# The second products of an expert layer turned: w2 stationary, 512 tokens moving, and the sum over experts kept transposed

## The chip, the cores and the metric

The kernel runs on one core of one Trainium2 chip. The metric is device time in microseconds (us), the median of the runs of one kernel. Engines carry the profile's names: PE is TensorE, DVE VectorE, ACT ScalarE, POOL GpSimd, SP the engine that issues most transfers.

## The reference

Three layers follow one another. The change touches the middle one, a mixture of E = 8 experts over N = 3072 tokens of width D = 384, with an inner width F = 1024; the gates P come from eight rounds of row and column scaling.

```python
def _moe_ref(x, w_gate, w1, w2):
    logits = x @ w_gate
    P = np.exp(logits - logits.max())
    for _ in range(8):
        P /= P.sum(1, keepdims=True) + 1e-09
        P /= P.sum(0, keepdims=True) + 1e-09
        P *= N / E
    for e in range(E):
        h = np.maximum(x @ w1[e], 0.0)
        ye = h @ w2[e]
        out += P[:, e:e + 1] * ye
```

Ahead of it stands a decaying linear attention (4 x 8 heads, 768 steps, head size 48), whose output is x; behind it a bilinear layer, `(x @ w_a) * (x @ w_b) @ w_out`, with an inner width of 1536.

## The kernel before

Every large product is made of float32 halves: an operand is split into a high part (a copy rounded to `F32R`) and a low part (the rest), and three matmuls high x high, high x low, low x high are added in PSUM.

The program has two parts. In the first, the attention of 24 steps of 128 tokens runs, and the gaps on PE are filled with expert 0 (`expert0`, seven of its eight 128-wide blocks, 256 tokens at a time, twelve batches); its result goes to DRAM as `y0`. In the second part, six phases of 1024 tokens follow: three of the expert layer (phases 0, 1, 2, here called the MoE phases) and three of the bilinear layer. An MoE phase has 19 jobs. A job takes three 128-wide blocks of the inner width through both products:

- `front` makes h = relu(x @ w1) for 2 x 512 tokens by a fast scheme of fifteen chains of three matmuls (w1 stationary, 512 tokens moving, line 975). Partial results are copied out of PSUM by ACT or combined by DVE (`pG`, `pF`, `z`).
- `halve` splits h into its two parts (`er`); ACT writes the high part, DVE or POOL the low one.
- `back` makes h @ w2 for all blocks of one expert that are pending, 22 calls a phase. Here h is stationary (128 x 128) and w2 moves (384 columns), so that the result has tokens on partitions: eight tiles of 128 tokens, each 3 matmuls a block (`gemm_t`, line 348, PSUM tile `pR`, three banks). DVE then adds it to `acc`, with the gate as a scalar of its partition (`scalar=prob[:, t, e:e+1]`).
- The accumulators start as `y0` times the gate of expert 0 (ACT). After the last expert, `x2` transposes each `acc` tile on PE (three matmuls), ACT copies it, and it goes to DRAM as `xd[1]` for the bilinear layer.

POOL splits the weights of the first product in phase 0 (`w1_split`, later phases load the split weights from DRAM), does part of the `halve` work, and makes sums of x (`x_make`). DVE also converts the float64 weights of the bilinear layer (`convert`, 60 pieces of seven DVE operations; `CONVERTS` says which jobs do how many). The gates (`sinkhorn`) are made at the start of phase 0, between its first products.

All work of the second part goes into a `Plan`: each piece has a priority, an engine, a cost by hand and the keys that it reads and writes, and the order on each engine is fixed by playing these through before the program is built. Engines take their own instructions strictly in that order.

Of the kernel before, what the change touches and what calls it, by code (L numbers as in the profile page):

```python
# [189 lines left out]
def kernel(  # L190
# [479 lines left out]
    def expert0(plan, b, prio, nm, bufs, fill, part=None):  # L670
# [20 lines left out]
        ws = ftiles(w_e0[0][1]) + ftiles(w_e0[1][1])  # L691
        for tt in range(EB // 128) if part != 0 else ():
# [28 lines left out]
    def sinkhorn(plan, prio, rounds, bank):  # L721
# [161 lines left out]
    def x_take(plan, prio, ph, i, eng, tmp):  # L883
# [6 lines left out]
        plan.add(prio + 5, ACT, .6, [kt, *(guard[:1] if i >= NX - 5 else [])], [f"xs{i}"], partial(nc.scalar.activation, out=xh, in_=t, func=AF.Copy))  # L890
# [19 lines left out]
    used.update(F=0, R=0)  # L910
# [4 lines left out]
    b_z = ring("z", 19, [128, TB], sbb)  # L915
# [3 lines left out]
    cut["at"] = sum(2 * KD * 128 * m for m in e0_f)  # L919
# [4 lines left out]
    acc = ring("acc", TPG, [128, DM], sbb)  # L924
# [24 lines left out]
    most = {(0, 1), (0, 2), (1, 1), (1, 2)}  # L949
    on_pool = {"moe": ({(1, 2)}, most, most), "out": ((), most | {(0, 0), (1, 0)}, most | {(0, 0), (1, 0)})}  # L950

    def front(n):
# [258 lines left out]
```

## Time and profile before

| | |
|---|---|
| median of 3 runs | 2205.8 us (2205.55 to 2208.18) |
| profiled execution, span | 2207.7 us (no time of its own is given beside the span; it lies inside the runs) |
| PE busy | 2173.2 us, 98% |
| DVE busy | 1613.6 us, 73% |
| ACT busy | 942.6 us, 43% |
| POOL busy | 906.7 us, 41% |

Busy shares are means over stages with different limits. A busy PE means that a matmul is in flight, since matmuls overlap; how fast they follow one another is read from starts in the timeline. The first part (attention and the fill) ends at 425.6 us; the MoE phases start at 425.6, 867.2 and 1318.2 us, the bilinear layer at 1766.2 us, each with the first matmul of its first job.

### The profile page before, as it was taken

The page shows a single profiled execution, that of the slowest core. Times are in us where ns is not written, and L with a number is a line of the kernel's source. Part 1 is how long each engine was busy: PE and PEld are TensorE (multiplying, and loading weights), DVE is VectorE, ACT ScalarE, POOL GpSimd, SP SyncE. Part 2 cuts the span into 40 slices and gives each one's busy share as a digit, 9 for nine tenths or more (in the row PEclk, how much of TensorE's full clock was granted, in tenths as well). Part 3 has the DMA queues.
Part 4 walks back from the last instruction along what each step waited for, and adds up shares of the span by engine and source line. Part 5 has one row for each costly group of instructions (what it writes and reads, how often), then busy time and mean ns, then how long its engine had stood idle before and what let it go on. Part 6 is the DMA issues. An engine that isn't in the chain of part 4 may idle for free.

```text
span 2207.7 us, 41959 instructions
## 1 busy us (share of the span) xinstructions
PE 2173.2 (98%) x15933; PEld 1967.3 (89%) x15933; DVE 1613.6 (73%) x2904; ACT 942.6 (43%) x1785; POOL 906.7 (41%) x921
## 2 busy tenths in 40 slices
PE   8999999989999999999999999999999999999999
PEld 8999999969899999889999998899999988888888
DVE  6878888387778778767786687777766866776755
ACT  3444454454444444533334345333333545433432
POOL 2212121277776665332322244343222677444512
PEclk9999999999999999999999999999999999999999
DMA  7556663466665557864544558666544546787642
GB/s 133 109 104 162 165 126 81 135 216 220 222 229 184 203 194 278 299 231 141 194 152 152 175 203 275 210 222 211 176 138 162 163 172 226 254 276 229 235 164 72
DMA packets 325354, 413.43 MB, mean 187 GB/s; under 512 B 146976, under 2 KB 217248, under 8 KB 321696
## 3 DMA queue, kind: packets, MB, share of 16 engines
q1 hardware_dynamic: 302832, 393.97, 55.9%
q10 hardware_dynamic: 22320, 16.78, 2.3%
q8 instruction: 125, 2.05, 0.4%
q14 instruction: 77, 0.63, 0.1%
HBM read 279.33 MB, written 126.62 MB: 184 GB/s over the span
## 4 chain that ended last, share of the span: by engine, by line
PE 85%; DVE 5%; DMA 4%; POOL 3%; issue 1%; SPq 1%; ACT 1%; ACTq 0%; POOLq 0%; DVEq 0%
PE pR L348 35%; PE pG L975 24%; PE pF L975 9%; PE pM L336 4%; PE pM L348 3%; PE pT L462 1%; POOL stage L1170 1%; DVE z L1170 1%; PE pA L505 1%; PE pO L590 1%; PE pO L618 1%; DMA stage<-in_moe_w_dram 1%; PE pA L549 1%; PE pA L517 1%; DVE er L1170 1%
## 5 line engine op out<-in xcount | busy, mean ns | idle before, releaser
L348 PE MATMUL pR<-er 128*128 128x384 f32 x5052 | 1022.5, 338 | 1.6 <-ACT l L686 1.1
L348 PEld LDWEIGHTS pR<-er 128*128 128x128 f32 x5052 | 907.5, 189 | 75.5 <-ACT l L686 1.5
L1170 POOL TENSOR_TENSOR er<-z,er 128x512 fp32r<-128x512 f32 x221 | 294.7, 1347 | 655.8 <-ACT er L1170 396.5
L1170 ACT ACTIVATE z<-pG 128x512 f32<-128x512 f32 x474 | 282.7, 597 | 577.9 <-PE pG L975 452.1
L975 PE MATMUL pG<-xsh,w 128*128 128x512 f32 x1134 | 440.9, 395 | 7.9 <-ACT z L1170 6.6
L1170 DVE SCALAR_TENSOR_TENSOR acc<-pR,prob,acc 128x384 f32<-128x384 f32 x528 | 319.4, 612 | 113.3 <-PE pR L348 111.0
L1170 ACT ACTIVATE er<-z 128x512 fp32r<-128x512 f32 x420 | 250.6, 626 | 222.8 <-PE pR L348 167.9
L1170 DVE TENSOR_TENSOR z<-pF,z 128x512 f32<-128x512 f32 x324 | 221.6, 687 | 121.4 <-PE pF L975 82.9
L975 PE MATMUL pG<-er,w 128*128 128x512 f32 x972 | 278.8, 396 | 3.5 <-DVE z L1170 3.4
L1170 DVE TENSOR_TENSOR z<-z,pG 128x512 f32<-128x512 f32 x243 | 166.6, 686 | 125.3 <-PE pG L975 121.8
L975 PEld LDWEIGHTS pG<-xsh,w 128*128 128x128 f32 x1134 | 212.7, 188 | 45.3 <-ACT z L1170 11.7
L975 PE MATMUL pG<-xsl,w 128*128 128x512 f32 x567 | 224.1, 395 | 0.0
L975 PEld LDWEIGHTS pG<-er,w 128*128 128x128 f32 x972 | 179.0, 188 | 28.8 <-DVE z L1170 6.8
L688 POOL TENSOR_TENSOR er<-l,er 128x256 fp32r<-128x256 f32 x84 | 75.2, 897 | 281.1 <-ACT l L686 248.8
L1170 DVE TENSOR_TENSOR z<-pG,z 128x512 f32<-128x512 f32 x174 | 119.7, 688 | 84.8 <-PE pG L975 82.0
L1170 DVE SCALAR_TENSOR_TENSOR er<-z,er 128x512 fp32r<-128x512 f32 x171 | 166.7, 981 | 6.0 <-ACT er L1170 3.2
L1170 POOL TENSOR_TENSOR stage<-stage 128x128 f32<-128x128 f32 x325 | 160.1, 524 | 25.7 <-DMA stage<-in_moe_w_dram 17.2
L1170 POOL TENSOR_TENSOR w<-stage,w 128x768 fp32r<-128x768 f32 (+2 forms) x75 | 124.2, 1664 | 73.2 <-ACT w L1170 73.2
L975 PE MATMUL pF<-er,w 128*128 128x512 f32 x486 | 139.4, 395 | 0.8 <-POOL er L1170 0.5
L975 PE MATMUL pF<-xsh,w 128*128 128x512 f32 x324 | 128.0, 397 | 2.0 <-DVE acc L1170 1.3
L306 POOL TENSOR_TENSOR er<-raw,er 128x384 fp32r<-128x384 f32 (+1 forms) x82 | 91.4, 1122 | 93.4 <-ACT er L304 93.2
L975 PEld LDWEIGHTS pG<-xsl,w 128*128 128x128 f32 x567 | 106.4, 188 | 7.8
(153 smaller groups left out, 2595.3 us busy)
## 6 DMA issues: line engine op xcount, KB each, us to landing
er<-w2d SPq DMA_DIRECT2D x138, 384.0 KB, 5.5
wfmoe<-w SPq DMA_DIRECT2D x19, 1920.0 KB, 7.3
w<-wfmoe SPq DMA_DIRECT2D x38, 768.0 KB, 5.1
w2d<-er SPq DMA_DIRECT2D x69, 384.0 KB, 4.4
w<-wfmoe SPq DMA_DIRECT2D x38, 640.0 KB, 4.5
w<-wfmoe SPq DMA_DIRECT2D x38, 512.0 KB, 4.1
wfout<-w SPq DMA_DIRECT2D x8, 1920.0 KB, 7.3
raw<-in_moe_w_dram SPq DMA_DIRECT2D x64, 192.0 KB, 3.0
```

Of the source, the lines that this page charges most:

```text
L306: plan.add(prio + 1, "POOL", .1 + m * .0026, [gk, key], [key], lambda: nc.gpsimd.tensor_tensor(out=lj, in0=got, in1=f32(hj), op=ALU.subtract))
L336: nc.tensor.matmul(out=ps, lhsT=a[:, kk, fs], rhs=b[:, kk, :], start=(i == 0), stop=(i == 3 * KD - 1),)
L348: nc.tensor.matmul(out=ps, lhsT=a[:, off:off + 128], rhs=b, start=(start and i == 0), stop=(stop and i == n - 1))
L462: nc.tensor.transpose(ps[0:R, p * 128:p * 128 + 128], src[:, p * 128:p * 128 + R], ident)
L505: nc.tensor.matmul(out=A0[o:o + 64, w, :], lhsT=pct(bk)[r, g, :], rhs=pct(bq)[r, g, :])
L517: nc.tensor.matmul(out=A1[o:o + 56, 0, w, :].rearrange("j (b e) -> j b e", e=8), lhsT=pct(k3)[r, g, 0:56], rhs=qv[r, g, :, 1, :])
L549: nc.tensor.matmul(out=A1[o:o + 48, 1, w, :].rearrange("j (b e) -> j b e", e=16), lhsT=pct(k3)[r, g, 0:48], rhs=qv[r, g, :, 1, :])
L590: nc.tensor.matmul(out=ps[64 * hd:64 * hd + m, p * D:(p + 1) * D], lhsT=kn[64 * c:64 * c + 64, p * R + 64 * hd:p * R + 64 * hd + m], rhs=b ...
L618: nc.tensor.matmul(out=o, lhsT=Y[w, c, p, :], rhs=X[w, 2 * p + c, :], start=True, stop=first and c == 0)
L688: op(POOL, .76, [f"hh{ft}", kf], [f"hl{ft}"], lambda hh=hh, hl=hl, hf=hf: nc.gpsimd.tensor_tensor(out=hl, in0=hf, in1=f32(hh), op=ALU.subt ...
L975: nc.tensor.matmul(out=ps, lhsT=a[:, slot], rhs=b, start=(new and i == 0), stop=(i == 2), skip_group_check=not new)
L1170: fn()
```

## The change

In all three MoE phases the second product is turned. w2 is stationary (128 x 128, three column groups d) and 512 tokens of h move, so that the result stands transposed: the inner width D on partitions, tokens in the free dimension. A block then has 2 halves x 3 d x 3 matmuls of 512 columns in place of 8 tiles x 3 matmuls of 384. The same is done for expert 0 in the first part, with 256 tokens moving.

The gate is no longer a scalar of a partition. It becomes a tile of 128 equal rows, loaded from a DRAM copy of the transposed gates (`pd`) by a broadcast transfer, one for each expert and half. DVE multiplies `pR` by it into one of two `tmp` tiles; a second addition, `acc += tmp`, is done by DVE or, for the pairs in `add_on_pool`, by POOL (three of six in phase 0, all in phase 1, two of six in phase 2). For expert 0, DVE adds `pR` to `acc` and POOL multiplies by the gate. `acc` leaves for DRAM as it stands: `x2` is not called any more in these phases. The `z` ring has 16 tiles in place of 19, the split sum of x number 9 now lies where expert 0's weights lay, and `CONVERTS` starts at job 2 of phases 1 and 2.

```diff
+    def gemm_d(ps, hs, ws, d, start=True, stop=True):
+        n = 3 * len(hs)
+        i = 0
+        for (hh, hl), (wh, wl) in zip(hs, ws):
+            for a, b in ((wh, hh), (wh, hl), (wl, hh)):
+                nc.tensor.matmul(
+                    out=ps, lhsT=a[:, d * 128:d * 128 + 128], rhs=b, start=(start and i == 0), stop=(stop and i == n - 1)
+                )
+                i += 1
...
-    b_z = ring("z", 19, [128, TB], sbb)
+    b_z = ring("z", 16, [128, TB], sbb)
+    b_tmp = ring("tmp", 2, [128, TB], sbb)
...
+    b_pb = [(f"pb{n}", t) for n, t in enumerate(ring("pb", 1, [128, TB], sbb) + [f32(er_take(TB))] + ring("pc", 1, [128, TB], sbb))]
...
+    add_on_pool = ({(0, 0), (0, 2), (1, 1)}, every, {(0, 0), (1, 1)})
...
+        for h in range(2):
+            kp, pb = pb_of[g, e][h]
...
+            for d in range(KD):
+                prio = start + step * (KD * h + d)
+                kr, ps = take("R", p_R)
...
+                    plan.add(prio + LATER_PE + part[0] * step // 4, PE, .227 * 3 * len(part), [x[0] for x in hp + wp],
+                             [kr, *(x[0] for x in stores if (h, d) == (0, KD - 1))], partial(
+                                 gemm_d, ps, [x[1:] for x in hp], [x[1:] for x in wp], d, part is parts[0], part is parts[-1]))
...
+                if e == 0:
+                    plan.add(prio, DVE, .69, [kr], ka, partial(tt, out=at, in0=ps, in1=at, op=ALU.add))
+                    plan.add(prio, POOL, 1.35, [kp], ka, partial(nc.gpsimd.tensor_tensor, out=at, in0=at, in1=pb, op=ALU.mult))
+                else:
+                    kz, z = take("Z", b_tmp)
+                    plan.add(prio, DVE, .69, [kr, kp], [kz], partial(tt, out=z, in0=ps, in1=pb, op=ALU.mult))
+                    if (h, d) in add_on_pool[g]:
+                        plan.add(prio, POOL, 1.35, [kz], ka, partial(nc.gpsimd.tensor_tensor, out=at, in0=at, in1=z, op=ALU.add))
+                    else:
+                        plan.add(prio, DVE, .8, [kz], ka, partial(tt, out=at, in0=at, in1=z, op=ALU.add))
...
-    CONVERTS = {(0, u): 1 for u in range(3, 19, 2)} | {(p, u): 1 + (u % 3 == 2 or u == 9) for p in (1, 2) for u in range(19)}
+    CONVERTS = {(0, u): 1 for u in range(3, 19, 2)} | {(p, u): 1 + (u % 2 == 0) for p in (1, 2) for u in range(2, 19)}
```

PE in the middle of phase 0, before: second products (line 348, 384 columns) stand between first products (line 975, 512 columns).

```order
1709 L348 MATMUL pR_6466<-er 128x384 x6
1710 L975 MATMUL pF_6461<-xsh_79,w_84 128x512
1711 L975 MATMUL pF_6461<-xsl_80,w_84 128x512
1712 L975 MATMUL pF_6461<-xsh_79,w_84 128x512
1713 L348 MATMUL pR_6464<-er 128x384 x6
```

The same engine and place after the change; line 362 is the turned second product, line 1029 the first product.

```order
1709 L362 MATMUL pR_6698<-er 128x512 x6
1710 L1029 MATMUL pG_6691<-er,w_83 128x512 x3
1711 L1029 MATMUL pG_6692<-xsh_75,w_84 128x512
1712 L1029 MATMUL pG_6692<-xsl_76,w_84 128x512
1713 L1029 MATMUL pG_6692<-xsh_75,w_84 128x512
1714 L362 MATMUL pR_6697<-er 128x512 x6
```

Between the two lists every 384-column matmul has gone; all matmuls of the stretch have 512 columns.

DVE in phase 0, before: each `pR` tile is taken by one operation that multiplies by the gate and adds to `acc`.

```order
1002 L1170 SCALAR_TENSOR_TENSOR acc_6496<-pR_6466,prob,acc_6496 128x384
1003 L1170 TENSOR_TENSOR z_6472<-z_6472,pG_6459 128x512
1004 L1170 SCALAR_TENSOR_TENSOR er<-z_6479,er 128x512
1005 L1170 SCALAR_TENSOR_TENSOR acc_6497<-pR_6464,prob,acc_6497 128x384
1006 L1170 SCALAR_TENSOR_TENSOR acc_6498<-pR_6465,prob,acc_6498 128x384
```

DVE in phase 0 after the change; `tmp<-pR,pb` (or `pc`, `er`: the three gate tiles) is the multiplication, `acc<-acc,tmp` the addition.

```order
1016 L1276 TENSOR_TENSOR tmp_6716<-pR_6698,pc_6727 128x512
1017 L1276 TENSOR_TENSOR tmp_6715<-pR_6696,pc_6727 128x512
1018 L1276 TENSOR_TENSOR acc<-acc,tmp_6716 128x512
1019 L1276 SCALAR_TENSOR_TENSOR er<-z_6710,er 128x512
1020 L1276 TENSOR_TENSOR tmp_6716<-pR_6697,pc_6727 128x512
1021 L1276 SCALAR_TENSOR_TENSOR er<-z_6709,er 128x512
1022 L1276 TENSOR_TENSOR acc<-acc,tmp_6716 128x512
```

A `pR` tile now takes one operation with `pR` as an input and, for half of the tiles of this phase, one more with both inputs in SBUF.

POOL at the start of phase 0 after the change: the six multiplications of expert 0 by the gate stand in the middle of the sums that make the split w1 (`stage`, `w`).

```order
67 L1276 TENSOR_TENSOR stage<-stage 128x128 x7
68 L1276 TENSOR_TENSOR acc<-acc,pb_6726 128x512 x3
69 L1276 TENSOR_TENSOR acc<-acc,er 128x512 x3
70 L1276 TENSOR_TENSOR acc<-acc,tmp_6715 128x512
71 L1276 TENSOR_TENSOR stage<-stage 128x128 x6
72 L1276 TENSOR_TENSOR acc<-acc,tmp_6715 128x512
73 L1276 TENSOR_TENSOR w_83<-stage,w_83 128x512
```

None of the `acc` rows was on POOL before; the sums and `w` rows behind them now come after the gate tiles have arrived.

## Rows read from the trace of the kernel before

**Rows 1.** The page: engines' busy time, share and instructions.

```profile
PE 2173.2 (98%) x15933; PEld 1967.3 (89%) x15933; DVE 1613.6 (73%) x2904; ACT 942.6 (43%) x1785; POOL 906.7 (41%) x921
```

**Rows 2.** Windows of first part, phases 0, 1, 2: length, then busy by engine.

```profile
core 0: us, PE busy (x) PEld busy (x) DVE busy (x) ACT busy (x) POOL busy (x), PEclk, DMA share, GB/s
0.00:425.60 425.60, 415.25 (x7119) 385.62 (x7120) 325.30 (x788) 195.31 (x466) 86.80 (x103) 1.00 0.56 120
425.60:867.20 441.60, 430.62 (x2169) 386.43 (x2168) 337.56 (x539) 202.12 (x369) 309.50 (x373) 1.00 0.61 218
867.20:1318.20 451.00, 446.87 (x2260) 405.83 (x2259) 335.46 (x583) 182.95 (x319) 138.22 (x112) 0.99 0.58 198
1318.20:1766.20 448.00, 445.45 (x2261) 405.47 (x2260) 326.66 (x575) 187.28 (x324) 162.26 (x130) 1.00 0.59 194
```

**Rows 3.** Windows of the steady middle of phases 0, 1 and 2.

```profile
523.00:844.60 321.60, 319.42 (x1613) 289.80 (x1612) 241.16 (x361) 142.17 (x253) 228.69 (x284) 1.00 0.58 207
970.60:1247.70 277.10, 277.10 (x1409) 253.06 (x1408) 202.38 (x359) 106.29 (x181) 74.20 (x64) 1.00 0.50 170
1417.00:1693.70 276.70, 276.70 (x1406) 252.65 (x1405) 199.21 (x356) 106.14 (x181) 86.28 (x65) 1.00 0.56 185
```

**Rows 4.** Phase 1's window, lines 975 and 348 alone: PE, PEld, clock, DMA.

```profile
970.60:1247.70 277.10, 149.53 (x542) 99.59 (x541) 1.00 0.50 170
970.60:1247.70 277.10, 175.79 (x867) 155.26 (x867) 1.00 0.50 170
```

**Rows 5.** PE timeline, 512- and 384-column matmuls in turn: start, us, instructions.

```profile
495.09 0.39 PE L975 MATMUL pG<-xsh,w 128*128 128x512 f32 x1
...
495.79 2.26 PE L348 MATMUL pR<-er 128*128 128x384 f32 x12
497.89 0.39 PE L975 MATMUL pG<-xsh,w 128*128 128x512 f32 x1
```

**Rows 6.** PE timeline, first and last of 18 matmuls of 512 columns.

```profile
464.63 0.84 PE L975 MATMUL pG<-er,w 128*128 128x512 f32 x3
...
468.48 0.39 PE L975 MATMUL pG<-xsh,w 128*128 128x512 f32 x1
```

**Rows 7.** PE timeline, matmuls of 256 columns, and what follows them.

```profile
434.42 2.31 PE L336 MATMUL pR<-er 128*128 128x256 f32 x18
436.57 0.40 PE L975 MATMUL pG<-xsh,w 128*128 128x512 f32 x1
```

**Rows 8.** Groups by line and shape: busy us, mean ns, idle before.

```profile
L1170 DVE SCALAR_TENSOR_TENSOR acc<-pR,prob,acc 128x384 f32<-128x384 f32 x528 | 319.4, 612 | 113.3 <-PE pR L348 111.0
L1170 POOL TENSOR_TENSOR er<-z,er 128x512 fp32r<-128x512 f32 x221 | 294.7, 1347 | 655.8 <-ACT er L1170 396.5 <-PE pR L348 230.4 <-PE pG L975 26.6
L1170 DVE TENSOR_TENSOR z<-pF,z 128x512 f32<-128x512 f32 x324 | 221.6, 687 | 121.4 <-PE pF L975 82.9 <-ACT z L1170 32.6
```

**Rows 9.** DVE instructions on z: shortest, median and longest in ns.

```profile
L1170 DVE TENSOR_TENSOR z<-pF,z x228: 671/691/694, 435.2 to 1764.3; 128x512 f32<-128x512 f32 x114
L1170 DVE SCALAR_TENSOR_TENSOR er<-z,er x168: 674/693/2340, 472.2 to 1762.1; 128x512 fp32r<-128x512 f32 x168
```

**Rows 10.** Windows of phases 0 and 2, tile er alone: PE, PEld, DVE, ACT, POOL.

```profile
425.60:867.20 441.60, 329.76 (x1631) 290.36 (x1631) 88.61 (x89) 93.33 (x173) 90.97 (x80) 1.00 0.61 218
1318.20:1766.20 448.00, 348.86 (x1724) 309.92 (x1722) 35.88 (x40) 72.83 (x123) 105.65 (x80) 1.00 0.59 194
```

**Rows 11.** Steady windows, tile acc alone: PE, PEld, DVE, ACT.

```profile
523.00:844.60 321.60, 0.00 (x0) 0.00 (x0) 71.19 (x117) 0.00 (x0) 1.00 0.58 207
970.60:1247.70 277.10, 0.00 (x0) 0.00 (x0) 64.59 (x106) 0.00 (x0) 1.00 0.50 170
1417.00:1693.70 276.70, 0.00 (x0) 0.00 (x0) 64.27 (x106) 0.00 (x0) 1.00 0.56 185
```

**Rows 12.** The transposes of x2, line 1096: shortest, median, longest in ns.

```profile
L1096 PE MATMUL pR<-ident,acc x72: 270/272/328, 898.2 to 1826.3; 128*128 128x128 f32 x72
```

**Rows 13.** Windows of single jobs in which DVE is busiest.

```profile
774.70:799.00 24.30, 23.94 (x122) 21.61 (x121) 22.19 (x33) 10.91 (x20) 14.68 (x18) 1.00 0.56 204
1739.30:1766.20 26.90, 26.90 (x139) 24.61 (x138) 25.75 (x39) 15.30 (x28) 23.31 (x26) 1.00 0.54 171
```

**Rows 14.** DVE timeline: the last gate operation, and the first use of gates.

```profile
485.00 1.14 DVE L756 TENSOR_TENSOR prob<-prob,sk_c 128x192 f32<-128x192 f32 x1
...
487.87 0.60 DVE L1170 SCALAR_TENSOR_TENSOR acc<-pR,prob,acc 128x384 f32<-128x384 f32 x1
```

**Rows 15.** DMA issues: number, KB each, median us from issue to landing.

```profile
wd<-z ACTq DMA_DIRECT2D x36, 128.0 KB, 2.5
l<-x2d SPq DMA_DIRECT2D x45, 256.0 KB, 3.7
```

More of the change, by code (lines that the diff above doesn't have):

```diff
@@ L691, in expert0 @@
         ws = ftiles(w_e0[0][1]) + ftiles(w_e0[1][1])
+        if part != 0 and b * EB // (2 * TB) in TURNED:
+            for d in range(KD):
+                km, psm = take(nm, bufs)
+                for n0 in range(4):
+                    n = min(2, NF0 - 2 * n0)
+                    hk = [f"h{x}{ft}" for ft in range(n0 * 2, n0 * 2 + n) for x in "hl"]
+                    fs = slice(n0 * 2, n0 * 2 + n)
+                    wk = [f"e0o{n0 // 2}{x}" for x in range(e0_f[n0 // 2])]
+                    op(PE, .36 * n, hk + wk, [km, "E0o"], partial(
+                        gemm_d, psm[:, :EB], hs[fs], ws[fs], d, n0 == 0, n0 == 3), 0.0, fill)
+                ys, ky = b_yt[d], f"l{1 + d % 2}"
+                op(ACT, .37, [km], [ky], lambda psm=psm, ys=ys: nc.scalar.activation(
+                    out=ys, in_=psm[:, :EB], func=AF.Copy))
+                op(ACT, .35, [ky], [], lambda ys=ys, d=d: nc.scalar.dma_start(
+                    out=y0t[d, :, b * EB:b * EB + EB], in_=ys), 3.0)
+            return
         for tt in range(EB // 128) if part != 0 else ():
@@ L719, with sinkhorn @@
                       oh[:, n], ol[:, n])
-    def sinkhorn(plan, prio, rounds, bank):
+    def sinkhorn(plan, prio, rounds, bank, tmp):
         def op(eng, cost, reads, writes, fn, late=0.0):
@@ L763, in sinkhorn, with turn @@
                 op(DVE, 1.45, [], ["r", "P"], rows, .5)
+        def turn():
+            for x in range(2):
+                m = min(128, NTILE * E - 128 * x)
+                nc.tensor.transpose(ps[0:m, 128 * x:128 * x + 128], flat_p[:, 128 * x:128 * x + m], ident)
+        kz, z = tmp
+        op(PE, .35, ["P"], [kp], turn)
+        for x in range(2):
+            m = min(128, NTILE * E - 128 * x)
+            zx, px = z[0:m, 128 * x:128 * x + 128], ps[0:m, 128 * x:128 * x + 128]
+            op(ACT, .3, [kp], [kz], partial(nc.scalar.activation, out=zx, in_=px, func=AF.Copy))
+            op(SP, .36, [kz], ["pd"], partial(nc.sync.dma_start, out=pd[128 * x:128 * x + m], in_=zx), 3.0)
     for i in range(NSTEP):
@@ L909 @@
     plan = Plan(.4, 1.5)
-    used.update(F=0, R=0)
+    used.update(F=0, R=0, Z=0)
     LATE = 5.0
@@ L923, with acc_keys @@
     w2s = [[t[:, x] for x in range(2)] for t in w2t]
-    acc = ring("acc", TPG, [128, DM], sbb)
+    acc_all = sbb.tile([128, TPG * DM], F32, name="acc")
+    acc = [acc_all[:, DM * j:DM * j + DM] for j in range(TPG)]
+    acc_t = [[acc_all[:, TB * (KD * h + d):TB * (KD * h + d + 1)] for d in range(KD)] for h in range(2)]
+    def acc_keys(lo, hi):
+        return [f"ac{x}" for x in range(lo // 128, hi // 128)]
+    pb_of = {}
+    b_pb = [(f"pb{n}", t) for n, t in enumerate(ring("pb", 1, [128, TB], sbb) + [f32(er_take(TB))] + ring("pc", 1, [128, TB], sbb))]
     l_of = [(f"l{n}", t) for n, t in enumerate(b_l)]
@@ L1034, in back @@
         kind, g = phases[ph]
+        turned = kind == "moe" and g in TURNED
         ws, stores = [], []
@@ L1049, in back @@
             add_piece(plan, at, f"w2{m}", [(0, 128, src)], wh, wl, [] if kind == "moe" else ["wd2"], LATE, .42)
+        if turned:
+            back_turned(ph, e, blocks, ws, stores, start, length, last)
+            return
         step = length // TPG
```

65 lines of the change are left out of this document (49 added, 16 removed).

## The prediction

> **What bounds the kernel now.** I read the busy shares first: TensorE is busy 98% of the span, VectorE 73% [rows 1]. Such a share is a mean, so the windows by phase come next. In the three MoE phases TensorE is busy 98 to 99% of the time, and VectorE 73 to 76% [rows 2]. In the steady middle of phases 1 and 2 it has no idle time at all: 277.10 us busy of 277.10 [rows 3]. So there a job lasts as long as its matmuls take to follow one another, and nothing else matters until an engine gets late enough to stop TensorE. Phase 0 differs in one thing: GpSimd is busy 70% of it, against 31 and 36% later [rows 2], since it splits w1 there.
>
> The rate is read from starts. Three matmuls of 512 columns between shorter ones take 0.70 us, 0.233 each; the twelve of 384 behind them 2.10 us, 0.175 each [rows 5]. Where only 512s follow one another, 17 steps take 3.85 us, 0.2265 each [rows 6]. The counts confirm it: phase 1's window holds 542 matmuls of 512 and 867 of 384 columns [rows 4], 542 x 0.233 + 867 x 0.175 = 278.0 us, measured 277.1.
>
> **The change, part by part.**
>
> *Rate of the second products.* 24 matmuls of 384 columns a block become 18 of 512: the same 9216 columns, three quarters of the instructions. The 867 in phase 1's window become 650, and with the shorter ones gone the stretch is all 512s: (542 + 650) x 0.2265 = 270.0 us, 7.1 less than 277.1. A phase has 57 blocks, three phases 171 x 24 = 4104 such matmuls, so the gain is 7.1 x 4104 / 867 = 34 us. The bounds: nothing, if the 512s stay at 0.233 (1192 x 0.233 = 278); 38 us, if the model's 278 is taken as the base. I take 34, because the new order has no shorter matmul in these stretches, as in rows 6.
>
> A rule is worth weighing here. The Trainium skill (TensorE: Matmul & The Clock Gate, Back-to-back issue gap) prices a matmul at its columns over 2.4 GHz plus 2.5 ns, so 24 x 162.5 against 18 x 215.8 ns, 0.016 us a block, 3 us in all: by it, turning the product is worth almost nothing. The rows disagree: 384 and 512 columns stand 15 and 13 ns above their columns at the full clock, not 2.5 [rows 5, 6].
>
> *x2 falls away.* 72 transposes on TensorE [rows 12]. Their spacing in a stream is not above that of 256-column matmuls, 18 of which take 2.15 us, 0.119 each [rows 7]: 72 x 0.119 = 8.6. Bounds 0 and 72 x 0.272 = 20 us; I take 8.
>
> *Expert 0 in the first part.* Per batch 42 matmuls of 384 become 63 of 256: 63 x 0.119 = 7.5 against 42 x 0.175 = 7.35 us, twelve times 0.17, 2 us lost (0 to 4).
>
> *VectorE and GpSimd.* One operation of 0.612 us on a 384-wide tile [rows 8] was all that the sum over experts cost. Now a multiplication with one PSUM input (0.687, as z<-pF,z [rows 8]) and, for part of the tiles, an addition with both inputs in SBUF. That addition has no row, but one like it has: the low part of h, er<-z,er. It takes 0.693 us in the median and up to 2.34, while an operation with a PSUM input never exceeds 0.694 [rows 9]. Its mean is 88.61 / 89 = 0.996 us in phase 0 and 35.88 / 40 = 0.897 in phase 2 [rows 10], where GpSimd is busy 70 and 36%. By these slopes I price the addition at 1.09 us in phase 0 (GpSimd then at 92%) and 0.95 in phase 2; bounds 0.69 and 2.03 (a whole GpSimd operation of 1.347 ahead of it).
>
> The Trainium skill says why (SBUF — State Buffer, Who interferes with whom): a VectorE instruction with two SBUF inputs contends with a GpSimd instruction that reads SBUF, one with a single SBUF input does not, and the loser blocks for the other's whole length. It speaks against this change, which makes 147 such additions on VectorE and 249 more reading operations on GpSimd; by it an addition that always finds GpSimd at work would cost the upper bound. The measured mean in phase 0 is a quarter of the way there.
>
> The load in the steady windows: phase 0 has 117 / 8 = 14.6 calls of the sum [rows 11], so 88 multiplications and 44 additions on each engine. VectorE: 241.2 - 71.2 + 88 x 0.687 + 44 x 1.09 + 7 (its 70 other two-SBUF operations at 1.09 instead of 0.996) = 285 of 313 us, 91% [rows 3, 11]. GpSimd: 228.7 + 44 x 1.347 = 288 of 313, 92% [rows 3, 8]. Phase 2: 199.2 - 64.3 + 79.5 x 0.687 + 53 x 0.95 = 240 of 270, 89%. Phase 1, where GpSimd does all additions: VectorE 192 of 270, 71%, GpSimd 74.2 + 79.5 x 1.347 = 181, 67%. So nothing is over 100%, but phases 0 and 2 come close. What that costs TensorE is bounded by single jobs with such a load today: at VectorE 91% TensorE idles 0.36 of 24.3 us (1.5%), at 96% not at all [rows 13]. These are single jobs; over whole phases the buffers do not carry it, so I take the full 1.5% of phases 0 and 2, 13 us.
>
> *Start of phase 0.* The gates are final at 486.1 us and first used at 487.9 [rows 14]. Now they must be transposed, stored and loaded again: some 1 us on TensorE and ScalarE, then a store and a load like wd<-z and l<-x2d, 2.5 and 3.7 us to landing [rows 15], about 8 to 9 us with issue. On VectorE this is covered: expert 0's six additions need no gate, and some twenty operations (14 us at 0.7) stand between the last gate operation and the first multiplication. On GpSimd it is not: expert 0's multiplications wait for the gate tile, and behind them stand the six sums and three splits that make w1 for a later job. I price that at 4 us (0 to 9).
>
> *At nothing:* ScalarE loses 24 scalings and 24 copies, but is 45% busy. The 48 gate tiles of 256 KB meet transfer engines at a share of 0.50 to 0.61 [rows 2, 3]; each is called for about half an expert ahead. Were one late, the multiplication, then the three pR banks, then TensorE would wait. Three z tiles fewer, with no z needed for x2 any more, and the conversions moved by two jobs, I price at nothing as well.
>
> Sum: -34 - 8 + 2 + 13 + 4 = -23. The profiled execution has 2207.7 us, 1.9 above the median of the runs, so 2184.7 there and **2183 us** as a median. By phase: 428 us for the first part, about 441, 437 and 441 for phases 0, 1 and 2, and 439 behind them.
>
> **The rivals.**
> 1. *Full gain:* the 13 and the 4 do not appear, since rows 13 has a job at 96% without a stall. 2207.7 - 40 - 1.9 = 2166.
> 2. *GpSimd holds phase 0, a little:* GpSimd waits 93 of the 321.6 us in phase 0's window today [rows 3]. With 288 us of work, TensorE's 313 leave room for 25. The additions wait for VectorE and VectorE for one of only two tmp tiles, so waits chain: GpSimd late, tmp not free, multiplication late, pR bank not free. If it keeps half of its waits, the window is 288 + 46 = 334, the phase 459 instead of 441, the time 2201.
> 3. *The same chain, slower than before:* keeping two thirds, 288 + 62 = 350, the phase 481, the time 2223. It decides from a little over half of today's waits. For it: engines in strict order and 92% load. Against it: an engine that is late finds its inputs ready, so most of today's waits (396 of 656 us on ScalarE's high part [rows 8]) should vanish.
> 4. *No rate gain:* the 512s stay at 0.233. TensorE being slower, the stalls halve: 0 - 8 + 2 + 6 + 4 = +4, 2210. Against it stand rows 6; and the rule of the Trainium skill on the issue gap, above, would end near here too.
>
> **How the numbers follow.** Forecast 0.56 (2172 to 2195), full gain 0.17, rival 2 0.11, rival 3 0.10, rival 4 0.06. A difference under 0.2% (about 4 us) can't be told from no change in this kernel. Faster takes the forecast, the full gain and most of rival 2: 0.80. Slower takes rival 3 and most of rival 4: 0.15. Same: 0.05. The range reaches from the full gain with the model's 38 us (2160) to rival 2 with some of rival 4 (2208); rival 3 and a little on the low side are left out.
>
> **What would show it.** Right: pR has 3078 matmuls of 512 columns in the MoE phases, following one another at 0.226 to 0.228 us, and so do the first products there, while the bilinear layer keeps 0.233 and 0.175. VectorE is near 90% in phases 0 and 2 and near 71% in phase 1, and its acc<-acc,tmp has a mean near 1.09 and 0.95. Phase 1 is the cleanest: it should be 13 to 15 us shorter. Wrong: TensorE's idle time in phase 0 above some 20 us, with pR waiting for VectorE and VectorE's tmp operations waiting for GpSimd; GpSimd idle on the gate tile for over 9 us near its start, and w late behind it; 512s that stay at 0.233; or a first part longer by more than 4 us.

## The result

The changed kernel takes 2238.3 us (median of 4 runs, 2235.4 to 2239.9) against 2206.9 us of the kernel before (4 runs, 2205.6 to 2208.2): ratio 1.0147, 95% interval 1.0131 to 1.0162. It is 31 us slower, where 2183 us was forecast. In the rows of after and of the experiments, L1029 is the line of the first products (L975 before), L362 that of the turned second products, L294 to L302 are the conversions of float64 weights (L291 to L299 before), and L1276 (L1282, L1281) is the plan's line for all other work.

The page of after, busy time by engine ([rows 1] of before):

```profile
PE 2159.8 (97%) x15089; PEld 1826.5 (82%) x15089; DVE 1790.9 (80%) x2919; ACT 933.3 (42%) x1751; POOL 1301.9 (58%) x1170
```

Windows of after: the first part, phases 0, 1, 2 and the bilinear layer ([rows 2]):

```profile
0.00:429.30 429.30, 419.82 (x7350) 394.87 (x7351) 321.94 (x789) 198.00 (x478) 87.99 (x104) 0.99 0.56 121
429.30:883.00 453.70, 428.87 (x1889) 342.85 (x1888) 405.69 (x547) 200.49 (x359) 415.26 (x428) 0.99 0.62 215
883.00:1338.10 455.10, 436.82 (x1882) 353.99 (x1882) 364.20 (x545) 177.42 (x301) 309.34 (x234) 0.98 0.64 206
1338.10:1791.30 453.20, 436.25 (x1885) 354.80 (x1884) 390.06 (x600) 180.84 (x303) 255.23 (x188) 0.99 0.62 200
1791.30:2237.40 446.10, 438.03 (x2089) 380.03 (x2087) 308.96 (x442) 176.54 (x311) 234.06 (x219) 1.00 0.60 206
```

The bilinear layer before, which [rows 2] does not show:

```profile
1766.20:2207.70 441.50, 435.03 (x2132) 383.95 (x2130) 288.66 (x421) 174.92 (x312) 209.92 (x204) 1.00 0.59 203
```

Read the length of a stretch against TensorE's busy time behind it. In the three MoE phases TensorE is busy 1301.9 us; before it was 1322.9 [rows 2]. So TensorE's busy time did fall by 21 us. But it is idle 60.1 us of these phases, where it was idle 17.7: 42 us more. VectorE is busy 160 us longer than before in these phases, and GpSimd 370 us. Phase 1, which was to be 13 to 15 us shorter, is 4 us longer. Against the forecast by phase the first part is 1 us longer, the MoE phases 13, 18 and 12, the bilinear layer 7.

The rate itself is as forecast. On TensorE's timeline of after, first and last of 43 matmuls of 512 columns:

```profile
1102.20 1.52 PE L362 MATMUL pR<-er 128*128 128x512 f32 x6
...
1111.72 0.62 PE L1029 MATMUL pG<-er,w 128*128 128x512 f32 x2
```

42 steps in 9.52 us are 0.2267 us each. Groups of after by line and shape ([rows 8, 9, 11] show their like):

```profile
L1276 DVE TENSOR_TENSOR z<-pF,z 128x512 f32<-128x512 f32 x324 | 218.2, 682 | 58.3 <-ACT z L1276 30.2 <-PE pF L1029 25.2 <-issue 0.6
L1276 DVE SCALAR_TENSOR_TENSOR er<-z,er 128x512 fp32r<-128x512 f32 x171 | 202.5, 1188 | 6.5 <-ACT er L1276 6.3
L1276 DVE TENSOR_TENSOR acc<-acc,tmp 128x512 f32<-128x512 f32 x147 | 160.5, 1093 | 1.0
L1276 POOL TENSOR_TENSOR acc<-acc,tmp 128x512 f32<-128x512 f32 x231 | 325.9, 1414 | 229.3 <-DVE tmp L1276 226.2 <-DMA l<-xf3d 1.8 <-DMA xf1d<-l 0.7
```

Operations with a PSUM input cost what they did (0.682 us). Those with both inputs in SBUF do not. The low part of h has a median of 1.078 us, where it was 0.693 [rows 9]; the first operation of a conversion, which has one SBUF input and no PSUM input, went the same way. Shortest, median and longest, of after and then of before:

```profile
L1276 DVE SCALAR_TENSOR_TENSOR er<-z,er x167: 673/1078/2325, 473.9 to 1768.7; 128x512 fp32r<-128x512 f32 x167
L294 DVE TENSOR_SCALAR z<-z x60: 242/704/1928, 495.5 to 1781.9; 128x256 int32<-128x256 int32 x36, 128x192 int32<-128x192 int32 x24
```

```profile
L291 DVE TENSOR_SCALAR z<-z x60: 247/284/1357, 498.6 to 1739.1; 128x256 int32<-128x256 int32 x36, 128x192 int32<-128x192 int32 x24
```

What TensorE waited for, of after and then of before (in all, times, longest):

```profile
PE pG L1029 <- DVE z L1276: 26.1, 25, 3.3
PE pR L362 <- DVE tmp L1276: 12.2, 11, 4.7
PE pG L1029 <- ACT z L1276: 7.0, 7, 2.4
PE pF L1029 <- DMA w<-wfmoe: 4.3, 3, 2.2
PE pG L1029 <- POOL w L1276: 3.5, 6, 1.7
```

```profile
PE pG L975 <- ACT z L1170: 6.6, 7, 2.2
PE pG L975 <- DVE z L1170: 3.4, 5, 1.6
```

The largest new wait is not behind the second products (`pR`), where the change was made, but behind the first: their two `pG` banks are emptied by VectorE and ScalarE, and the late one is mostly VectorE.

### The profile page after: what moved, and what is told of

Read it like the earlier page. It is cut to its first block, busy times and chain, and to the rows that moved or that the text cites. A ratio compares the mean times of both kernels' runs of the same rounds, so it can differ in the third digit from the quotient of the medians.

```text
span 2237.4 us, 40498 instructions
## 1 busy us (share of the span) xinstructions
PE 2159.8 (97%) x15089; PEld 1826.5 (82%) x15089; DVE 1790.9 (80%) x2919; ACT 933.3 (42%) x1751; POOL 1301.9 (58%) x1170
## 5 line engine op out<-in xcount | busy, mean ns | idle before, releaser
L362 PE MATMUL pR<-er 128*128 128x512 f32 (+1 forms) x3204 | 802.0, 389 | 15.4 <-DVE tmp L1276 12.2
L362 PEld LDWEIGHTS pR<-er 128*128 128x128 f32 x3204 | 596.7, 190 | 148.6 <-DVE tmp L1276 19.6
L1276 ACT ACTIVATE z<-pG 128x512 f32<-128x512 f32 x474 | 282.5, 597 | 575.9 <-PE pG L1029 433.9
L1276 POOL TENSOR_TENSOR acc<-acc,tmp 128x512 f32<-128x512 f32 x231 | 325.9, 1414 | 229.3 <-DVE tmp L1276 226.2
L1029 PE MATMUL pG<-xsh,w 128*128 128x512 f32 x1134 | 438.8, 397 | 20.9 <-DVE z L1276 10.2
L1276 POOL TENSOR_TENSOR er<-z,er 128x512 fp32r<-128x512 f32 x221 | 305.1, 1388 | 205.6 <-ACT er L1276 175.1
L1276 ACT ACTIVATE er<-z 128x512 fp32r<-128x512 f32 x420 | 258.3, 629 | 241.8 <-PE pR L362 147.6
L1029 PE MATMUL pG<-er,w 128*128 128x512 f32 x972 | 276.8, 394 | 16.1 <-DVE z L1276 15.9
L1029 PEld LDWEIGHTS pG<-xsh,w 128*128 128x128 f32 x1134 | 214.1, 189 | 76.7 <-ACT z L1276 14.7
L1276 DVE TENSOR_TENSOR z<-pF,z 128x512 f32<-128x512 f32 x324 | 218.2, 682 | 58.3 <-ACT z L1276 30.2
L1276 DVE TENSOR_TENSOR z<-z,pG 128x512 f32<-128x512 f32 x243 | 165.4, 682 | 89.3 <-PE pG L1029 88.5
L1029 PEld LDWEIGHTS pG<-er,w 128*128 128x128 f32 x972 | 179.5, 188 | 60.2 <-DVE z L1276 27.0
L1029 PE MATMUL pG<-xsl,w 128*128 128x512 f32 x567 | 222.8, 393 | 0.0
L1276 DVE SCALAR_TENSOR_TENSOR er<-z,er 128x512 fp32r<-128x512 f32 x171 | 202.5, 1188 | 6.5 <-ACT er L1276 6.3
L1276 POOL TENSOR_TENSOR stage<-stage 128x128 f32<-128x128 f32 x325 | 176.9, 575 | 10.8 <-DMA stage<-in_moe_w_dram 6.8
L351 PE MATMUL pR<-er 128*128 128x384 f32 x864 | 172.6, 337 | 0.0
L351 PEld LDWEIGHTS pR<-er 128*128 128x128 f32 x864 | 154.5, 188 | 11.6 <-DVE er L1276 0.2
L1276 DVE TENSOR_TENSOR acc<-acc,tmp 128x512 f32<-128x512 f32 x147 | 160.5, 1093 | 1.0
L1276 DVE TENSOR_TENSOR z<-pG,z 128x512 f32<-128x512 f32 x174 | 119.2, 686 | 45.9 <-PE pG L1029 44.3
L1276 POOL TENSOR_TENSOR w<-stage,w 128x768 fp32r<-128x768 f32 (+2 forms) x75 | 129.9, 1739 | 18.7 <-ACT w L1276 16.7
L1029 PE MATMUL pF<-er,w 128*128 128x512 f32 x486 | 138.5, 393 | 1.5 <-DVE z L1276 1.3
```

Source lines behind the costliest of these rows:

```text
L351: nc.tensor.matmul(out=ps, lhsT=a[:, off:off + 128], rhs=b, start=(start and i == 0), stop=(stop and i == n - 1))
L362: nc.tensor.matmul(out=ps, lhsT=a[:, d * 128:d * 128 + 128], rhs=b, start=(start and i == 0), stop=(stop and i == n - 1))
L1029: nc.tensor.matmul(out=ps, lhsT=a[:, slot], rhs=b, start=(new and i == 0), stop=(i == 2), skip_group_check=not new)
L1276: fn()
```

## The experiments

Two theories were to be told apart. *Collisions:* an addition on GpSimd reads SBUF and lengthens VectorE's instructions that run beside it. *Queue:* GpSimd or VectorE simply has too much to do, and the chain over the two `tmp` tiles holds `pR` (rivals 2 and 3). A third suspect came from the trace of after: the borders between phases. "Job" is the mean distance of job starts in the steady middle of a phase (13 jobs, in phase 2 beginning one job earlier), worked out from the starts of the first products: before 22.97, 23.05 and 23.14 us in phases 0, 1, 2; after 23.78, 22.54 and 22.98. The forecast of 34 us alone would make it 22.4.

**Which phases are turned.** `turned_none` keeps every edit beside the turning.

```diff
-    TURNED = (0, 1, 2)
+    TURNED = ()          # turned_none; (1,) turned_1; (1, 2) turned_12
```
```diff
+    TURNED = (1, 2)      # turned_12_pool
-    add_on_pool = ({(0, 0), (0, 2), (1, 1)}, every, {(0, 0), (1, 1)})
+    add_on_pool = ({(0, 0), (0, 2), (1, 1)}, every, every)
```

> TURNED = (): all other edits of the change stay (16 z tiles, two tmp and three gate tiles allocated, conversions from job 2 on, split sum number 9 moved, gates transposed and stored), but every second product is as before. If the side edits cost the 30 us (rival): 2225 to 2240 us. If the turned products themselves do (theory: VectorE and GpSimd late in phases 0 and 2, acc stored and reloaded between phases): 2203 to 2213, as before.

> TURNED = (1, 2): phase 0 and its share of expert 0 as before, phases 1 and 2 turned. Theory (VectorE and GpSimd too loaded in phase 0): phase 0 falls from 454 back to 440 to 444 us and the time to 2218 to 2226, the rest of the loss staying at the borders of phases. Rival (the loss lies at the borders of phases and not in phase 0): 2230 to 2240.

> TURNED = (1, 2), and all additions of phase 2 on GpSimd as in phase 1. Theory: phase 2's steady jobs fall from 22.9 to 22.5 us, as in phase 1, and the time lies 5 to 9 us under turned_12. Rival (additions do not matter, conversions and borders do): within 2 us of turned_12.

> TURNED = (1,): only the phase in which GpSimd makes all additions and VectorE has room is turned. The rate gain of its steady jobs is 0.5 us a job, some 7 to 9 us; against it the border to phase 2. Theory (load and collisions of phases 0 and 2 were the loss): 2196 to 2206, faster than before by up to 0.5%. Rival (borders cost what a phase gains): 2206 to 2216.

Measured: turned_none 2205.6 us, ratio 0.9998 [0.9986, 1.0011]; turned_1 2209.7, 1.0013 [1.0003, 1.0023]; turned_12 2213.7, 1.0028 [1.0012, 1.0045]; turned_12_pool 2244.8, 1.0177 [1.0148, 1.0206]. The fewer z tiles and the moved conversions cost nothing in all, but they move time between phases: phase 1 of turned_none takes 442 us and phase 2 455, before 451 and 448. That has to be taken off when turned_1 is read. There phase 1 takes 436 us and phase 2 behind it 460, so the turning itself gives some 6 us in phase 1 and takes 5 in phase 2; the total is in the range of the rival (borders cost what a phase gains). turned_12 came out better than either of its forecasts. More additions on GpSimd, which were to relieve VectorE and gain 5 to 9 us, made it 31 us worse: in the profiled executions, which lie 17 us apart, phase 2 went from 455 to 470 us and the layer behind it from 448 to 463. Why that layer grew is not shown.

**The additions left out.** Without a piece, the plan sets another order.

```diff
 # no_adds: neither; no_pool_adds: without the first; no_dve_adds: without the second
-    plan.add(prio, POOL, 1.35, [kz], ka, partial(nc.gpsimd.tensor_tensor, out=at, in0=at, in1=z, op=ALU.add))
-    plan.add(prio, DVE, .8, [kz], ka, partial(tt, out=at, in0=at, in1=z, op=ALU.add))
 # dve_all: all 378 on VectorE
+    add_on_pool = (set(), set(), set())
 # psum_adds: VectorE's additions read pR and acc, so that the gate is left out of those terms
+    plan.add(prio, DVE, .8, [kz, kr], ka, partial(tt, out=at, in0=ps, in1=at, op=ALU.add))
```

> All phases turned, the additions acc += tmp left out (147 on VectorE, 231 on GpSimd), so the sum over experts is not made; the multiplications stay. Theory (second addition and its collisions hold TensorE up): steady jobs at 22.4 to 22.6 us in all phases, TensorE idle in phase 0 down from 25 to under 12 us, time 2190 to 2205. Rival (borders of phases): steady jobs change by under 0.3 us, time 2220 to 2235.

> All phases turned; the 231 additions on GpSimd left out, the 147 on VectorE kept (the sum is incomplete). All additions together cost 57 us (no_adds). Theory A (GpSimd's share does it: it collides with VectorE's two-input operations, blocks its own queue and so the split of w1): 2195 to 2208, with phases 0 and 1 below 440 us and phase 2 near 448. Theory B (VectorE's own extra work does it): 2222 to 2235.

> All phases turned; the 147 additions on VectorE left out, the 231 on GpSimd kept (the sum is incomplete). Theory B (VectorE's load): phases 0 and 2 fall by 10 us or more each, phase 1, which has none of them, stays at 455; 2205 to 2215. Theory A: under 8 us gained, 2230 or more.

> All phases turned; all 378 additions on VectorE, none on GpSimd. VectorE's load in the steady jobs would be about 98% in phase 0, 90% in phase 1 and 95% in phase 2, with fewer collisions. Theory A (GpSimd's queue and its collisions are worse than VectorE's load): 2215 to 2232. Theory B: 2245 to 2280.

> All phases turned; VectorE's 147 additions read pR in PSUM and acc, instead of tmp and acc, so they have one SBUF input (the gate is left out of them). Theory C (collisions with GpSimd are what makes these additions dear): their mean falls from 1.09 to 0.69 us, 60 us of VectorE time go, and most of what no_dve_adds gains is gained here, 2212 to 2222. Rival (an operation more on VectorE is what costs, however long): 2230 to 2240.

Measured: no_adds 2180.6 us, 0.9879 [0.9855, 0.9904]; no_pool_adds 2194.4, 0.994 [0.992, 0.996]; no_dve_adds 2230.6, 1.0104 [1.0084, 1.0124]; dve_all 2270.6, 1.028 [1.0255, 1.0306]; psum_adds 2217.4, 1.0044 [1.0027, 1.0061]. So the additions cost 58 us together (more than either forecast of no_adds had), most of it (44 us) those on GpSimd. no_pool_adds (within 1 us) and no_dve_adds fit theory A. Without any, a job takes 22.38 and 22.39 us in phases 0 and 1, where the gain in rate is there in full, and 22.65 in phase 2. Leaving out VectorE's 147 gives only 8 us, although VectorE is then busy 124 us less (1666.5 us); letting them read PSUM gives 21. With all 378 on VectorE the time is 32 us over the change, in the range of theory B: VectorE's load is not free either. Each of these has an order of its own, so the pair of 8 and 21 us is not explained. What no_dve_adds waits for, and the sum of its three MoE phases, go against the load all the same:

```profile
PE pG L1029 <- DVE z L1276: 30.9, 21, 8.2
sum 1353.70, PE 1302.85 PEld 1062.30 DVE 1052.27 ACT 557.25 POOL 935.20; mean PE 434.28 PEld 354.10 DVE 350.75 ACT 185.75 POOL 311.73
```

The wait for VectorE ahead of `pG` is as long as in the change. `memset_adds`, the next group's second run, has VectorE just as busy in these phases, 1051.99 us, and waits 5.8 us there.

**The same order, with less reading.** These keep the order of all instructions on TensorE, VectorE and ScalarE, and of GpSimd's other instructions. In `hollow_adds` GpSimd's 231 additions cover 16 of 512 columns; in `memset_adds` GpSimd is as busy as in after, but with fills, which write SBUF and read nothing; in `no_reload` the loads of `y0t` into `acc` at the starts of phases 1 and 2 are left out. `hollow_no_reload` has the edits of the first and the third.

```diff
 # hollow_adds
-    plan.add(prio, POOL, 1.35, [kz], ka, partial(nc.gpsimd.tensor_tensor, out=at, in0=at, in1=z, op=ALU.add))
+    plan.add(prio, POOL, 1.35, [kz], ka, partial(nc.gpsimd.tensor_tensor, out=at[:, 0:16], in0=at[:, 0:16], in1=z[:, 0:16], op=ALU.add))
 # memset_adds, in place of the same line
+    def fill(at=at, z=z):
+        nc.gpsimd.tensor_tensor(out=at[:, 0:16], in0=at[:, 0:16], in1=z[:, 0:16], op=ALU.add)
+        for lo, hi in ((16, 512), (16, 512)):
+            nc.gpsimd.memset(at[:, lo:hi], 0.0)
+        nc.gpsimd.tensor_tensor(out=at[:, 0:16], in0=at[:, 0:16], in1=z[:, 16:32], op=ALU.add)
...
 # no_reload
-    nc.sync.dma_start, out=acc_t[h][d], in_=y0t[d, :, g * 2 * TB + h * TB:g * 2 * TB + (h + 1) * TB]), 9.0)
+    nc.sync.dma_start if g == 0 else (lambda **k: None), out=acc_t[h][d], in_=y0t[d, :, g * 2 * TB + h * TB:g * 2 * TB + (h + 1) * TB]), 9.0)
```

> As the change, in its order on every engine, but GpSimd's 231 additions cover 16 of 512 columns, so they take a tenth of the time (most of the sum is left out). Theory A (GpSimd's additions, by their time on GpSimd and at the port): about as no_pool_adds, 2192 to 2208. Rival (the order that the planner made with them is what costs): 2225 or more.

> As hollow_adds, but between a first and a last addition of 16 columns GpSimd writes zeros over the rest of acc with two memsets, about 1.2 us in all: GpSimd is occupied nearly as long as in the change, waits and releases as there, but reads almost nothing of SBUF. Theory A1 (the collisions with VectorE's two-input and conversion operations cost): VectorE's busy time falls by some 100 us and the time is that of hollow_adds within 8 us. Theory A2 (GpSimd's queue is late, and what stands behind the additions on it): time stays at 2228 or more.

> As the change, in its order, without the transfers of y0t into acc in phases 1 and 2 (the sums start on what acc held). Theory D (acc that has to be stored by SP before SP reloads it stops VectorE, then TensorE, at the borders of phases): 8 to 16 us faster than the change, from the stretches of jobs 18 to 23 and 37 to 41. Rival (the borders suffer from the conversions' and x's loads behind it in any case): within 4 us.

> Both suspects of the loss are taken away at once: GpSimd's 231 additions cover 16 of 512 columns, and the loads of y0t into acc at the starts of phases 1 and 2 are left out (the output is then not the layer's). Alone the two were worth 37 and 17 us. If they are separate losses, the time falls by both: 2238 - 37 - 17 = 2184 us, 1% under the kernel before and within 1 us of the forecast of 2183. If the long border stalls are themselves made by the crowded VectorE (the conversions that the border waits for are the ones that GpSimd lengthens), the second is contained in the first and the time stays at 2196 to 2201 us.

Measured: hollow_adds 2200.7 us, 0.9969 [0.9956, 0.9982]; memset_adds 2209.4, 1.0008 [0.9994, 1.0022]; no_reload 2220.8, 1.0067 [1.0047, 1.0087]; hollow_no_reload, both at once, 2184.8, 0.9894 [0.9879, 0.9909]. The page of memset_adds:

```profile
PE 2150.6 (97%) x15089; PEld 1828.2 (83%) x15089; DVE 1685.6 (76%) x2919; ACT 933.8 (42%) x1751; POOL 1299.3 (59%) x1863
```

GpSimd is busy 1299.3 us, in after 1301.9. VectorE does the same 2919 instructions in 105 us less. Its groups, and TensorE's wait behind `pG`:

```profile
L1282 DVE SCALAR_TENSOR_TENSOR er<-z,er x169: 673/704/2100, 476.7 to 1774.8; 128x512 fp32r<-128x512 f32 x169
L294 DVE TENSOR_SCALAR z<-z x60: 244/368/1927, 497.5 to 1753.3; 128x256 int32<-128x256 int32 x36, 128x192 int32<-128x192 int32 x24
```

```profile
PE pG L1029 <- DVE z L1282: 5.8, 8, 2.2
```

Of the 38 us that hollow additions give back, 29 come back when GpSimd merely stops reading. The order is the same and GpSimd is as busy, so this decides for the collisions; 9 us are left for the time that the additions hold GpSimd. TensorE is idle 57.5 us with the fills and 77.6 in the change, 20 us less, and the wait above falls by 20 us. The reload was worth 17 us, a little over the 8 to 16 expected. With it gone too, the loss is gone: -38 and -17 add up to 2183, and the two together measured 2184.8. They are separate losses. Windows of hollow_no_reload, phases 0, 1, 2:

```profile
427.90:863.30 435.40, 423.87 (x1889) 344.53 (x1888) 382.34 (x548) 199.28 (x358) 347.13 (x428) 0.99 0.64 225
863.30:1300.10 436.80, 430.09 (x1882) 353.41 (x1882) 315.80 (x544) 177.68 (x302) 181.06 (x233) 1.00 0.66 211
1300.10:1736.60 436.50, 430.24 (x1885) 352.61 (x1884) 360.32 (x599) 181.54 (x303) 190.01 (x187) 1.00 0.63 204
```

What the reload does is seen on the timeline of after at the border of phases 0 and 1. `acc` must first be stored (`x2d<-acc`), then loaded, both in SP's queue, and expert 0's sums wait for it. First what SP's queue waited for in all of after, then the timeline:

```profile
SPq L1276 <- DMA x2d<-acc: 32.4, 9, 7.0
```

```profile
955.84 0.59 SPq L1276 DMA_DIRECT2D x2d<-acc  x1
...
963.15 0.32 SPq L1276 DMA_DIRECT2D acc<-y0t  x1
963.35 0.76 PE L1029 MATMUL pG<-xsh,w 128*128 128x512 f32 x1 [2.44 <-ACT z L1276]
...
968.21 0.29 DVE L294 TENSOR_SCALAR z<-z 128x256 int32<-128x256 int32 x1 [9.09 <-DMA z<-in_moe_w_a_dram]
968.89 0.68 DVE L1276 TENSOR_TENSOR tmp<-pR,pb 128x512 f32<-128x512 f32 x1
968.90 0.33 SPq L1276 DMA_DIRECT2D acc<-y0t  x1
...
969.62 4.89 PE L362 MATMUL pR<-er 128*128 128x512 f32 x12 [4.66 <-DVE tmp L1276]
```

VectorE stands for 9.09 us at a conversion whose weights have not landed; the product that frees `pR` is behind it. SP issues in order, so the loads behind a held `acc<-y0t` go out late. With the loads of `acc` left out, SP's queue waits for those stores 2.1 us in place of 32.4, and VectorE for these weights 4.6 us in place of 9.1. The kernel before has no such wait; what makes the 4.6 us that stay was not tested.

**The gate folded into h.** If the extra addition is what costs, the products can be turned without it: GpSimd multiplies h by the gate before h is split, one PSUM sum holds all blocks of a job, even of two experts, and VectorE adds it to `acc` in one operation with one SBUF input. `y0t` comes through a z tile, not into `acc`. There are no `tmp` tiles then, and 18 z tiles.

```diff
+    plan.add(start + length // 2 * h - 500 + 60 * x, POOL if on else DVE, 1.35 if on else 1.0, [kp], [ky], partial(
+        nc.gpsimd.tensor_tensor if on else tt, out=z, in0=z, in1=pb, op=ALU.mult))
...
-    plan.add(prio, DVE, .69, [kr, kp], [kz], partial(tt, out=z, in0=ps, in1=pb, op=ALU.mult))
+    plan.add(prio, DVE, .69, [kr, kz], ka, partial(tt, out=at, in0=ps, in1=z, op=ALU.add))
 # fold_12: TURNED = (1, 2); fold_1: (1,); all six products of a job on GpSimd
 # fold_12_dve: TURNED = (1, 2), two of the six on VectorE
```

> Phases 1 and 2 turned, phase 0 as before; the gate is multiplied into h (GpSimd, 114 products a phase in place of 132 and 44 additions), so that one PSUM sum holds all blocks of a job and VectorE adds it to acc in one operation with one SBUF input: 114 a phase in place of 132 products and up to 88 additions. If the collisions and the two-input additions of VectorE are what cost (57 of the missing 55 us), phase 2 loses 84 us of additions on VectorE and gains 33 us of collisions (70 more GpSimd operations at 0.47 us), both phases come to 437 to 442 us, and the total to 2190 to 2200 us, under the kernel before. If the borders (store and reload of acc) decide, the time stays at the 2210 to 2214 us of the version that turns phases 1 and 2 unfolded.

> The same with phase 1 alone turned. Unfolded it measured 2209.7 us: phase 1 436 us in place of 451, phase 2 460 in place of 448, since phase 2 begins with another form of acc. If the collisions decide, phase 1 stays at 436 to 438 (GpSimd has 114 operations in place of 132) and the loss at the border shrinks only if it came from VectorE: 2200 to 2205 us. If the border's store and reload decide, 2208 to 2211 us.

> fold_12 with two of the six products of a job on VectorE and four on GpSimd. If a GpSimd operation costs VectorE 0.47 us, moving 38 products a phase gives 18 us back and takes 38 x 0.95 = 36 us: VectorE has 18 us a phase more, and the time is 0 to 8 us over that of fold_12. If GpSimd's own queue is what holds fold_12, it is faster than fold_12 instead.

Measured: fold_12 2207.4 us, 1.0002 [0.999, 1.0015]; fold_1 2215.7, 1.0042 [1.0025, 1.0059]; fold_12_dve 2201.1, 0.9966 [0.9955, 0.9978]. The last is 0.3% under the kernel before. In fold_12 and fold_12_dve the steady jobs have the full gain (22.38 and 22.45 us in phases 1 and 2; 22.40 and 22.23), but in fold_12 phase 1 takes 454 us: its first five jobs take 137 us, in fold_12_dve 130, before 127. Phase 2 is 441 us, as forecast. So fold_12 met neither of its forecasts, 2190 to 2200 and 2210 to 2214. What TensorE waited for in it, then in fold_12_dve:

```profile
PE pG L1029 <- ACT z L1281: 20.6, 16, 5.1
PE pG L1029 <- DVE z L1281: 8.1, 12, 1.5
```

```profile
PE pG L1029 <- DVE z L1281: 13.7, 11, 6.2
PE pG L1029 <- ACT z L1281: 8.5, 13, 1.4
```

Fewer products on GpSimd helped by 6 us where I had priced a loss of 0 to 8, so here GpSimd's queue seems to count: with all six there, ScalarE's instructions on `z` wait 76 us for GpSimd's, with four 50 us, and TensorE behind ScalarE waits longer. The two have orders of their own, so the 6 us are not shown to be that alone. fold_1 missed both forecasts: its bilinear layer takes 458 us, before 441. Its forecast took the long phase 2 of turned_1 for the border's; as said above, turned_none has most of that too.

## Why the prediction was wrong

*Rate of the second products, -34: right.* 0.2267 us a step against 0.2265 forecast; 22.38 us a job without additions against 22.4. The rule of the Trainium skill that allowed 3 us (TensorE: Matmul & The Clock Gate, Back-to-back issue gap) is given there for the gap of a single matmul by itself. For this stream it is not borne out: a 512 stands 13 ns above its columns at the full clock, as in [rows 6]. Rival 4 falls.

*x2, expert 0, edits at nothing: no sign against them.* turned_none, which has the edits but neither of the others, is within 0.2%. The first part grew by 3.7 us, where +2 was said, but ten traces with all phases turned have it at 426.6 to 431.6 us, so a single one does not tell 2 from 4. The 8 us of x2 were not measured by themselves.

*"VectorE and GpSimd", +13: this step failed; it measured over 50 us.* Leaving all additions out gives 58 back, and hollowing GpSimd's alone gives 38, which stand beside the 13. A job in phase 0 stands 1.4 us above the 22.38 without additions, 26 us over 19 jobs, where 1.5% (0.34 us) was taken; in phase 2 it stands 0.3 us above its 22.65, about as taken. The rest lies at the starts: the first five jobs of phase 1 take 140 us, without additions 131, the first four of phase 2 109 and 95, part of which is the border's. The sign set down for being wrong, TensorE idle for over 20 us in phase 0, came with 24.8. The step failed in two places.
- It priced the new additions (1.09 in phase 0 and 0.95 in phase 2; measured 1.27 and 0.95) and 7 us for the 70 like operations of phase 0. All else that meets GpSimd stayed at its old price. By the groups, the conversions grew from 209 to 263 us and the low parts of h from 194 to 232: 92 us where 7 were said. With hollow additions they are 200 and 199. Counted over the single instructions in the traces, by whether one of GpSimd's two-input operations was in progress at any time during them (mean us, number):

```
                              none in progress   one in progress
before  er<-z,er (STT)        0.689 x57          1.127 x114
after   er<-z,er (STT)        0.678 x17          1.245 x154
after   acc<-acc,tmp          0.694 x38          1.232 x109
after   L294, 256 columns     0.283 x4           0.910 x32
after   tmp<-pR,gate          0.682 x126         0.681 x252
after   z<-pF,z               0.684 x102         0.681 x222
```

- It asked whether VectorE's load stays under 100%, and took the price of a load near 90% from one job [rows 13]. The loads came out as forecast: 279.63 of 309.20 us (90%) in the middle of phase 0, 247.57 of 274.90 (90%) in phase 2; phase 1 has 79% where 71 was said. But TensorE's idle time in phase 0 was 4.1% where 1.5 was taken; only in phase 2, with 1.4%, did that price hold:

```profile
555.20:864.40 309.20, 296.42 (x1271) 237.25 (x1270) 279.63 (x353) 134.89 (x234) 295.27 (x307) 0.99 0.61 212
1022.60:1315.60 293.00, 291.99 (x1285) 240.66 (x1284) 231.31 (x363) 116.65 (x195) 193.94 (x152) 1.00 0.58 186
1447.50:1722.40 274.90, 270.94 (x1183) 222.43 (x1182) 247.57 (x395) 108.39 (x181) 131.87 (x95) 0.99 0.64 204
```

And no_dve_adds, with VectorE busy 124 us less, gained 8 us. What costs, as I read the waits, is that VectorE's short instructions before a `pG` copy take 1 to 2 us at the wrong moment: `pG <- DVE z` is 3.4 us before, 26.1 after, 30.9 in no_dve_adds, 5.8 with fills.

The rule cited for this (the Trainium skill, SBUF — State Buffer, Who interferes with whom) was used by half in the prediction. The same section also lists one-input kinds, tensor_scalar among them, that can run in a mode which contends with GpSimd; L294 agrees, 0.28 us alone and 0.91 beside GpSimd. And it says that a GpSimd instruction that only writes does not contend with a two-input one; the fills agree, a median of 0.704 against 1.078 us. The 37 low parts of h beside which a fill ran for more than 0.4 us have a mean of 0.697 us.

*Start of phase 0, +4: not told apart.* No run takes GpSimd's wait for the first gate tile away by itself. TensorE's waits for GpSimd's `w` are 5.8 us in all.

*The borders, not in the sum: 17 us.* Loading `acc` anew was there before too, but what went to DRAM was ScalarE's copy of the transposed tile, so the load had to wait for the transposes alone (7.8 us of SP's queue, 8 times). Without x2, `acc` itself is stored, and the load waits until the store has landed (32.4 us, 9 times). The prediction took x2's end for a pure gain and put this wait at nothing without a reason. The gate tiles of [rows 15]'s kind were weighed and were little trouble (6.7 us of VectorE's waits in two places).

*The rivals.* Rival 3 ended on the right side (2223), by the wrong mechanism: VectorE's `tmp` operations wait for GpSimd 22.3 us in all (13.7 for its additions), TensorE's wait for `tmp` is 12.2 us and stays at 10.5 when the additions are hollow, and GpSimd held as long by fills costs 9 us, not 40. Rival 2 has the same mechanism. By the terms, 2183 + 38 + 17 = 2238, measured 2238.3. That it is so close is partly luck: with both taken away phases 0 to 2 last 435, 437 and 437 us, where 441, 437 and 441 were forecast, and the bilinear layer 444, where 439 were.

*What stays open:* why leaving out VectorE's additions gains less (8 us) than letting them read PSUM (21 us), each with an order of its own; what made the bilinear layer longer, by 5 us in the change and most of all in fold_1; and how much of the border is the load and how much the strict queue behind it.

## What to carry to other kernels

When work moves to GpSimd, price it twice: its own time, and what it adds to the VectorE instructions beside it that have both inputs, or as in the conversions their only one, in SBUF. List all of those, not only the new ones; here 231 additions cost VectorE some 105 us, 0.45 us each. A load under 100% is no proof that an engine is on time: ask which short instruction stands ahead of a buffer that the bound engine waits for. And where an accumulator is stored and refilled between phases, the store, the load and what is queued behind them belong in the sum.

## What was not expected of the hardware

A short stop costs more than its length. Windows of after around the border: TensorE was busy 3.02 of 5.00 and 9.89 of 13.30 us, and then, behind a stop of 2.44 us, the granted clock is 0.51 for a stretch, the lower level of 1.2 GHz:

```profile
945.00:950.00 5.00, 3.02 (x12) 2.17 (x12) 5.00 (x10) 1.11 (x2) 1.95 (x2) 1.00 0.98 281
950.00:963.30 13.30, 9.89 (x39) 6.93 (x39) 5.30 (x10) 2.83 (x5) 8.37 (x7) 1.00 0.82 272
963.30:973.60 10.30, 5.59 (x12) 3.93 (x13) 4.43 (x9) 1.23 (x2) 3.17 (x3) 0.51 0.97 346
973.60:985.00 11.40, 11.00 (x47) 8.36 (x46) 7.45 (x13) 3.65 (x6) 7.74 (x6) 1.00 0.38 107
```

The twelve matmuls at 969.62 take 4.89 us, 0.4 each in place of 0.227. Summed from 300 us on, the trace of after has 34 us at the lower level and that of before 14; hollow_no_reload has 17. So stops of a few us at the borders also make the matmuls behind them slower. By the two spacings the 20 us more cost at most some 8 us of the 31, an estimate.
